# Storing the last tile's output in three parts (256, 128, 128 columns) in place of two (384, 128), in a retention and MLP kernel

## The chip, the cores and the metric

The kernel runs on one core of a Trainium2 chip. The metric is the device time of one execution in microseconds; the median of several executions is given. The profile is that of one further execution, seen by the hardware profiler.

## What is computed

Two layers follow each other. The first is a recurrent retention layer over 4 batches, 8 heads, 768 steps and 64 values a head; the second is a normalised two-matmul MLP with a residual, on 4 x 768 rows of 512 columns. Cut to what matters:

```python
for t in range(S):                                   # 768 steps
    state = gamma * state + einsum('bhd,bhe->bhde', k[:, :, t], v[:, :, t])
    y[:, :, t] = scale * einsum('bhd,bhde->bhe', q[:, :, t], state)
x  = y.transpose(0, 2, 1, 3).reshape(B, S, H * D)    # 4 x 768 x 512
xn = (x - mean(x)) / sqrt(var(x) + 1e-06) * g_ln
out = x + maximum(xn @ w_ch1, 0.0) @ w_ch2           # w_ch1 512 x 2048, w_ch2 2048 x 512
```

## The kernel before

The 3072 rows are cut into 24 tiles of 128 rows, numbered 0 to 23. The recurrence is not run step by step: inside a chunk of 128 steps it is a masked product of q and k, and a state for each chunk carries what went before. The weights are kept in bf16. A row's division by its standard deviation commutes with the MLP's matmuls and the maximum, so it is applied last, as `rstd`.

The order of all work is written out by hand in a long list, `ORDER`, of tokens that are emitted one after the other (the loop at L615). Each engine runs its own instructions in the order in which they are emitted, and waits by semaphores for what it needs from the others. A token such as `z23_1//Y1` means: step `z`, tile 23, part 1, into PSUM bank Y1. A step's engine stands behind the first slash; `st23/A` is a store that ScalarE's queue issues. The steps at the end of the list, around the change, are these:

- `z` (L543): the second matmul of the MLP. For a tile it accumulates 16 matmuls (`ho` 0 to 15) over the hidden 2048 values; each has a weight load of 128 x 128 of `h1` and streams columns `lo` to `hi` of `w2`. It is emitted in four parts of four matmuls.
- `ad` (L550): VectorE reads the bank, multiplies by `rstd`, adds the residual `x_all`, and writes one of six buffers `osb` (number `t + piece`, modulo 6).
- `st` (L557): a DMA, issued by ScalarE's queue, writes those columns of the buffer to the output.

All tiles but the last are one piece of 512 columns. The last tile, 23, is cut at the columns in `CFG["tail"]`; its pieces are written 23, 23b and (where there is a third) 23c in the tokens:

```python
CUTS = CFG["tail"]
COLS = {(t, 0): (0, DM) for t in range(NT - 1)}
COLS.update({(NT - 1, i): c for i, c in enumerate(zip(CUTS, CUTS[1:]))})
...
lo, hi = COLS[t, piece]                              # in z, ad and st alike
for ho in range(4 * part, 4 * part + 4):
    nc.tensor.matmul(bank(("m2", t, piece))[:, 0:hi - lo],
                     lhsT=slot(h1, t // 4)[:, ho, t % 4 * P:(t % 4 + 1) * P],
                     rhs=w2[:, ho, lo:hi], start=(ho == 0), stop=(ho == HO - 1))
```

At the end of the list before the change, TensorE's order is: part 0 of `z23` (bank Y1) in between parts of tile 22 (bank Y0), then tile 20 (bank PD), the last part of tile 21 (bank M), parts 1 to 3 of `z23`, and the 16 matmuls of `z23b` (bank PD). VectorE's is `ad20`, `ad22`, `ad21`, `ad23`, `ad23b`, and ScalarE issues the stores in that order too.

What closes the program is not in the list. Each DMA that SyncE's or ScalarE's queue issues gets one of eight completion counters, in turn (called counter 0 to 7 here). Before the change there are 64 such DMAs, eight for each counter. A DMA waits for the one before it on its counter. When all work is issued, SyncE waits (rows of L643) for these counters, one instruction after the other, in the order 0, 1, ... 7, each together with another semaphore; ahead of them stands one wait for GpSimd's counters. Then the engines meet in a barrier, the semaphores are cleared, and the program ends.

Of the kernel before, what the change touches and what calls it, by code (L numbers as in the profile page):

```python
# [15 lines left out]
 'TX': 8,  # L16
 'groups': [1, 1, 1, 1, 1, 1, 1, 1, 2, 2, 2, 2, 4, 4],
 'pairs': [(8, 9), (10, 11), (12, 13), (14, 15), (16, 17), (18, 19), (20, 21), (22, 23)],
 'tail': (0, 384, 512),
 'slots': {'state': 3,  # L20
           'k0': 7,
           'q0': 4,
# [69 lines left out]
r13_4/A r13_15/A st18/A m13_7//X2 r13_5/A m13_0//X1 r13_7/A m13_8//X0 r13_0/A st17/A st14/A  # L92
st16/A m13_11//X3 r13_8/A r13_11/A z22_0//Y0 m13_10//X2 z21_0//M z21_1 z22_1 r13_10/A z21_2
z22_2 z23_0//Y1 z22_3 z20_0//PD z20_1 z20_2 z20_3 z21_3 ad20 ad22 z23_1 st20/A ad21 z23_2 st22/A
z23_3 st21/A z23b_0//PD ad23 z23b_1 z23b_2 z23b_3 st23/A ad23b st23b/A
""".split()


# [549 lines left out]
```

## Time and profile before

| | |
|---|---|
| median of 3 runs | 211.5 us (210.9 to 212.0) |
| the profiled execution | 211.45 us |
| its span, first to last instruction | 209.7 us |
| TensorE (PE) busy | 202.2 us, 96% of the span |
| VectorE (DVE) busy | 127.7 us, 61% |
| ScalarE (ACT) busy | 76.7 us, 37% |
| GpSimd (POOL) busy | 95.4 us, 45% |
| stores of the output | 23 of 256 KB, one of 192 KB, one of 64 KB |

The span runs from the first to the last instruction of any engine; 1.8 us of the profiled execution's time lie around it. A busy TensorE is not one at its peak: its matmuls overlap, and the start of the next one tells more than the duration of one. SyncE (SP) is never counted as busy; its rows are those of a queue, as are the rows marked with a q behind the engine's name. Times of single rows, where they are given to the nanosecond, are from the trace's instruction and DMA records.

### The profile page before, as it was taken

How to read it: one execution, taken by the hardware profiler on the slowest of the kernel's cores; microseconds unless marked ns; L12 is line 12 of the kernel's file. 1: busy time of each engine (PE TensorE's matmuls, PEld its weight loads, DVE VectorE, ACT ScalarE, POOL GpSimd, SP SyncE). 2: the span in 40 equal slices, each digit the busy share in tenths (PEclk: the TensorE clock that was granted, in tenths of full speed). 3: DMA queues.
4: the chain of work that ended last, by engine and by line, in shares of the span. 5: the costliest groups of instructions: out<-in, count | busy, mean ns of one | idle time of the engine just before them, and what ended most of it. 6: DMA issues, size and time to landing. Idle time of an engine off the chain costs nothing.

```text
span 209.7 us, 4961 instructions
## 1 busy us (share of the span) xinstructions
PE 202.2 (96%) x2007; PEld 131.6 (63%) x2031; DVE 127.7 (61%) x297; ACT 76.7 (37%) x168; POOL 95.4 (45%) x145
## 2 busy tenths in 40 slices
PE   7989999999999999999999999999999999999994
PEld 3568999897558566576587676475545444444443
DVE  4797898596349858579695566978948403110023
ACT  6366654442400514415237124214372512346000
POOL 8997592792695796780587459500000000000000
PEclk9999999999999999999999999999999999999999
DMA  9999999999999999999999999966032400015005
GB/s 130 175 180 180 161 199 163 160 175 154 155 133 169 124 185 124 140 122 210 211 147 171 161 176 106 190 67 143 0 105 100 102 0 3 0 50 202 0 3 200
DMA packets 109946, 27.11 MB, mean 129 GB/s; under 512 B 102625, under 2 KB 106977, under 8 KB 109922
## 3 DMA queue, kind: packets, MB, share of 16 engines
q0 software_dynamic: 77024, 13.37, 87.6%
q1 hardware_dynamic: 28242, 6.85, 25.0%
q10 hardware_dynamic: 4656, 6.56, 10.0%
q8 instruction: 16, 0.26, 0.6%
q14 instruction: 8, 0.07, 0.1%
HBM read 27.30 MB, written 6.29 MB: 160 GB/s over the span
## 4 chain that ended last, share of the span: by engine, by line
PE 54%; DVE 4%; issue 1%
PE X L520 23%; PE M L543 16%; PE Y L543 6%; PE PD L543 4%; DVE trq L386 2%; PE X L395 2%; PE Y L423 1%; PE PD L465 1%; DVE state L475 1%; PE Y L401 1%; DVE osb L550 1%; DVE xn L441 0%; DVE rstd L513 0%
## 5 line engine op out<-in xcount | busy, mean ns | idle before, releaser
L520 PE MATMUL X<-xnt,w 128*128 128x128 bf16 (+2 forms) x896 | 93.8, 257 | 0.0
L531 ACT ACTIVATE h<-X 128x512 bf16<-128x512 f32 x89 | 51.0, 602 | 82.1 <-PE X L520 70.2
L520 PEld LDWEIGHTS <-w 128*128 128x128 bf16 x896 | 66.1, 98 | 20.5 <-issue 0.2
L543 PEld LDWEIGHTS <-h 128*128 128x128 bf16 x400 | 37.4, 98 | 38.2 <-issue 0.3
L543 PE MATMUL M<-w,h 128*128 128x512 bf16 x238 | 59.4, 379 | 1.5 <-issue 0.5
L408 DVE TENSOR_TENSOR asb<-X,mask 128x512 bf16<-128x512 f32 x48 | 30.6, 683 | 11.8 <-PE X L395 11.5
L457 POOL TENSOR_TENSOR vg<-v,vsc 128x512 bf16<-128x512 bf16 x20 | 20.9, 1049 | 9.0 <-DMA v<-in_v_dram 7.3
L550 DVE SCALAR_TENSOR_TENSOR osb<-M,rstd,x_all 128x512 f32<-128x512 f32 x16 | 11.9, 746 | 20.0 <-PE M L543 18.1
L447 ACT CAST x_all<-Y 128x256 bf16<-128x256 f32 (+1 forms) x39 | 14.4, 410 | 25.2 <-DVE xn L441 25.2
L337 POOL DMA_DIRECT2D v<-in_v_dram x24 | 21.9, 912 | 3.6 <-DMA w<-in_moe_w_ch_dram 1.6
L543 PE MATMUL Y<-w,h 128*128 128x512 bf16 (+1 forms) x93 | 21.7, 370 | 0.2
L431 DVE BATCH_NORM_STATS2 bns<-Y 128x6 f32<-128x256 f32 (+1 forms) x39 | 16.3, 454 | 8.2 <-PE Y L423 8.0
L441 DVE SCALAR_TENSOR_TENSOR xn<-Y,mv,gb 128x256 bf16<-128x256 f32 (+1 forms) x39 | 18.6, 512 | 1.2 <-PE Y L423 0.6
L475 DVE TENSOR_TENSOR state<-PD,gch 64x256 bf16<-64x256 f32 x40 | 16.6, 415 | 0.6 <-PE PD L465 0.3
L337 POOL DMA_DIRECT2D qk<-in_q_dram x17 | 15.2, 893 | 1.2 <-issue 1.1
L337 POOL DMA_DIRECT2D qk<-in_k_dram x17 | 15.3, 898 | 0.9 <-issue 0.8
L550 DVE SCALAR_TENSOR_TENSOR osb<-PD,rstd,x_all 128x512 f32<-128x512 f32 (+1 forms) x3 | 1.9, 618 | 20.1 <-remote 17.2
L386 DVE TENSOR_TENSOR trq<-tr,qsc 128x512 bf16<-128x512 bf16 x17 | 10.8, 643 | 3.5 <-DMA tr<-qk 3.3
L564 PE MATMUL PD<-zeros 128*128 128x512 bf16 (+1 forms) x32 | 8.5, 402 | 1.2 <-DVE zeros L250 1.2
L423 PEld LDWEIGHTS <-asb 128*128 128x128 bf16 x192 | 8.0, 98 | 2.7 <-DVE asb L408 0.9
L366 POOL COPY scrap<-qk 1x1 bf16<-1x1 bf16 x28 | 4.9, 176 | 9.8 <-DMA qk<-in_k_dram 8.5
L543 PE MATMUL PD<-w,h 128*128 128x512 bf16 (+1 forms) x46 | 8.4, 324 | 0.1
(75 smaller groups left out, 130.9 us busy)
## 6 DMA issues: line engine op xcount, KB each, us to landing
out_dram<-osb ACTq DMA_DIRECT2D x23, 256.0 KB, 2.4
w<-in_moe_w_ch_dram POOLq DMA_DIRECT2D x8, 512.0 KB, 8.6
v<-in_v_dram POOLq DMA_DIRECT2D x24, 128.0 KB, 6.3
qk<-in_k_dram POOLq DMA_DIRECT2D x17, 128.0 KB, 6.8
qk<-in_q_dram POOLq DMA_DIRECT2D x17, 128.0 KB, 5.7
k<-in_k_dram POOLq DMA_DIRECT2D x6, 128.0 KB, 7.6
q<-in_q_dram POOLq DMA_DIRECT2D x6, 128.0 KB, 7.6
tr<-qk SPq DMA_TRANSPOSE x17, 5.8
```

Source lines behind the costliest of these rows:

```text
L337: nc.gpsimd.dma_start(out=dst, in_=tok[kind][TILES[t]])
L386: nc.vector.tensor_tensor(out=slot(trq, t), in0=x, in1=qsc, op=ALU.mult)
L408: nc.vector.tensor_tensor(out=slot(asb, t)[:, :, par, :], in0=bank(("pa", t, par)).rearrange("p (i t) -> p i t", t=P), in1=mask.rearrange( ...
L431: nc.vector.bn_stats(out=bns[:, t, i, :], in_=x)
L441: nc.vector.scalar_tensor_tensor(out=dst, in0=src, scalar=mv[:, t, 0:1], in1=g, op0=ALU.subtract, op1=ALU.mult)
L447: nc.scalar.copy(out=dst, in_=src)
L457: nc.gpsimd.tensor_tensor(out=slot(vgs, chunk(t)), in0=v_of(t), in1=vsc[:, c, :].unsqueeze(2).to_broadcast([P, H, D]), op=ALU.mult)
L475: nc.vector.tensor_tensor(out=slot(state, chunk(t) - 1)[o, :, o], in0=pd[o, :, o], in1=gch[o, c - 1, :].unsqueeze(2).to_broadcast([D, NPAI ...
L520: nc.tensor.matmul(bank(("mm", g, ho))[:, j * n * P:(j + 1) * n * P], lhsT=w1[:, ko, (ho + j) * P:(ho + j + 1) * P], rhs=x[:, x0:x0 + n, k ...
L531: nc.scalar.activation(out=dst, in_=src, func=AF.Relu)
L543: nc.tensor.matmul(bank(("m2", t, piece))[:, 0:hi - lo], lhsT=slot(h1, t // 4)[:, ho, t % 4 * P:(t % 4 + 1) * P], rhs=w2[:, ho, lo:hi], st ...
L550: nc.vector.scalar_tensor_tensor(out=slot(osb, t + piece)[:, 0:hi - lo], in0=bank(("m2", t, piece))[:, 0:hi - lo], scalar=rstd[:, t:t + 1] ...
```

## The change

The last tile's columns are cut at 256 and 384 in place of 384 alone, and the list gets the steps of the third piece. `z23` has 256 columns then, `z23b` and `z23c` have 128 each. `z23c` accumulates in bank Y0, which tile 22 used before, and its matmuls follow those of `z23b` on TensorE. On VectorE `ad23c` follows `ad23b`, and on ScalarE's queue `st23c` follows `st23b`. `ad23c` writes buffer 1 of `osb`, which tile 19 used before. `st23c` is the 65th DMA of the counters in turn and gets counter 0. On GpSimd and in SyncE's work nothing is added, moved or taken away.

```diff
- 'tail': (0, 384, 512),
+ 'tail': (0, 256, 384, 512),
...
-z23_3 st21/A z23b_0//PD ad23 z23b_1 z23b_2 z23b_3 st23/A ad23b st23b/A
+z23_3 st21/A z23b_0//PD ad23 z23b_1 z23b_2 z23b_3 st23/A z23c_0//Y0 ad23b z23c_1 z23c_2 z23c_3
+st23b/A ad23c st23c/A
```

## The prediction

> **What bounds the kernel now.** I read the page first, then the chain of waits from its end backwards, then the last six microseconds engine by engine, and last the SyncE rows behind the end of the work.
>
> ```profile
> span 209.7 us, 4961 instructions
> PE 202.2 (96%) x2007; PEld 131.6 (63%) x2031; DVE 127.7 (61%) x297; ACT 76.7 (37%) x168; POOL 95.4 (45%) x145
> PEclk9999999999999999999999999999999999999999
> ```
>
> TensorE is busy throughout at the full granted clock. The chain that ended last says the same of the end:
>
> ```profile
> 203.87 1.95 PE Y L543 x12
> 205.82 0.91 PE PD L543 x16
> 206.72 0.02 issue
> 206.75 0.35 DVE osb L550
> ```
>
> Up to 206.7 the second matmul layer (`z`, L543) runs without a pause; the last add (`ad23b`, L550) follows its last matmul. The chain view stops there, but the span runs on to 209.65. The same stretch by windows (PE, PEld, DVE, ACT, POOL busy, granted clock, DMA share, GB/s):
>
> ```profile
> 205.65:206.71 1.06, 1.06 (x18) 0.88 (x15) 0.62 (x1) 0.00 (x0) 0.00 (x0) 1.00 0.99 381
> 206.71:207.13 0.42, 0.00 (x0) 0.00 (x0) 0.35 (x1) 0.00 (x0) 0.00 (x0) 1.00 0.09 29
> 207.13:208.74 1.61, 0.00 (x0) 0.00 (x0) 0.00 (x0) 0.00 (x0) 0.00 (x0) 1.00 0.48 163
> 208.74:209.70 0.96, 0.00 (x0) 0.00 (x0) 0.00 (x0) 0.00 (x0) 0.00 (x0) 1.00 0.00 0
> ```
>
> So the end has four terms in a row: the last matmuls, the add of 128 columns (0.42 with its hand-overs), the last store (1.61), and 0.96 in which no engine and no transfer works. That last one is SyncE's closing waits (L643) and the barrier behind them:
>
> ```profile
> L643 SPq EVENT_SEMAPHORE  x1: 28/28/28, 208.7 to 208.7; - x1
> L643 SPq DRAIN  x1: 13/13/13, 208.8 to 208.8; - x1
> ```
>
> In the trace's rows this last wait runs at 208.740, 17 ns after the last store's final landing mark (208.723); the next instruction starts at 208.807. It is the last of a list that asks for completion counter 0, 1, ... 7 in that order; today the last store owns counter 7, so nothing is left to ask for after it.
>
> **The change part by part.** The sum is made against the profiled execution: 211.45 us, its span 209.65 with 1.80 around it. The median of the runs shown is 211.5, so the two stand together.
>
> *TensorE.* Sixteen matmuls of 384 columns become sixteen of 256, and sixteen of 128 (`z23c`) come in behind `z23b`. Columns in total stay 8192. Start to start in the trace's rows: 162.5 ns for 384 columns (these sixteen), 109 ns for 256 (256 matmuls at L520), 56 ns for 128 (`z23b`). 16 x (109 + 56 - 162.5) = 40 ns. All of it lies on the path: the last matmul ends 0.04 later. The first four of the sixteen stand ahead of `z22_3`, so the adds of tiles 20 to 22 come 4 x 53.5 = 0.21 us earlier. What could go wrong is that thirty-two thin pairs of weight load and matmul in a row do not hold the pace of sixteen. The nearest rows are early in the kernel, where 143 thin matmuls in a row (most of them 128 columns wide, L520) start 54.3 ns apart on average between 30.1 and 37.8 us. Bounds for `z23c`: 16 x 54 = 0.87 below; above, one weight load's whole duration, 98 ns, for each matmul: 1.57, or 0.67 more. I take 0.90, since the rows are the same shape; a gain is excluded, as no column disappears.
>
> The Trainium skill, "TensorE: Matmul & The Clock Gate", section Back-to-back issue gap, speaks against this part: a stream of weight-load and matmul pairs is said to sustain about 81 ns a matmul at 128 columns, and about 131 at 512. This trace has 56 and 216 for the two, so it disagrees in both directions. By the page the sixteen new pairs would take 1.30 us and not 0.90, and the end would come 0.40 later still.
>
> *Does `z23c` wait?* Its bank Y0 was tile 22's, free when `ad22` ends at about 204.2 (204.45 now, less 0.21); `z23c` starts at about 205.7. The cover is 1.5 us of `z23_1` to `z23b`; without it TensorE, with nothing behind, would stand for the remainder. Cost nothing.
>
> *VectorE.* The profile's adds take 0.35 (128 columns), 0.62 (384) and 0.74 (512), about 0.133 per 128 columns, so 256 columns should take 0.48. `ad23` runs from about 205.0 to 205.5, behind `ad21`, which then ends at 204.9; `ad23b` from 205.9 to 206.25; `ad23c` from 206.79 to 207.14. Only the last is on the path, and it is as long as the last one now: 0. Its buffer's earlier store (tile 19) landed at 186.3, so its added wait is over 20 us early, and nothing is queued behind it on VectorE.
>
> *ScalarE's queue.* One more store is issued: `st23` (128 KB), `st23b` and `st23c` (64 KB each) at about 205.5, 206.3 and 207.17, each 0.34 long. They do not meet. `st23c` also waits for the previous owner of its completion counter, tile 17's store, landed at 192.4.
>
> *The last store.* It keeps its size and comes 0.04 later. From issue to its final mark it takes 1.59 now, with its first packets at 207.99 while the 192 KB store's last packet ends at 208.04: an overlap of 0.04. After the change the store ahead is 64 KB and 0.9 earlier, so that overlap goes. Bounds: -0.05 (the overlap and a little) and +0.05 (the marks of one store alone lie 0.18 apart). I take 0.
>
> *SyncE's closing waits.* This is the term that the diff does not show. The 64 transfers of the hardware queues take their completion counters in turn, eight each; the 65th, `st23c`, falls to counter 0. The closing list is unchanged, so the wait for counter 0 comes first among the eight and will hold SyncE until about 208.78 (208.74 + 0.04). Then seven more waits, all long satisfied, must still be run one by one. Satisfied waits on SyncE are in the trace:
>
> ```profile
> L380 SPq EVENT_SEMAPHORE  x2: 28/28/28, 85.9 to 86.0; - x2
> L380 SPq DMA_TRANSPOSE tr<-qk x1: 1470/1470/1470, 86.1 to 86.1; - x1
> ```
>
> Those two waits for two counters each, the form of the closing ones, start at 85.924 and 85.989, and the transpose behind them at 86.056: 65 and 67 ns. Seven at 65 are 0.455. Bounds from the quickest and slowest satisfied wait that I found, 49 ns (95.134 to 95.183, one counter) and 73 (73.549 to 73.622): 0.34 to 0.51. Nothing hides it, because every engine then waits at the barrier behind SyncE; before the change the same seven lie under the stores in flight. A gain is excluded, since the waits run in order.
>
> Sum: 0.04 + 0 + 0 + 0.455 = 0.50. From 211.45 this gives 211.9 us (211.95 unrounded), the span 210.15. That is 0.23% more. The fourth window, 0.96 now, grows to about 1.42; the earlier adds and stores buy nothing, since the end hangs on the last piece, which is as big as before.
>
> **The rivals.**
>
> *Closing waits cost nothing.* If SyncE's list were run otherwise at the end than at 85.9, or its rows overlapped the landing, only the 0.04 and the last store's -0.05 to +0.05 remain: 211.4 to 211.5. For it: the closing list has never been seen with its satisfied part behind the last landing. Against it: every satisfied wait in the trace takes 49 to 73 ns of SyncE's own time. Chance 0.14.
>
> *Slower: TensorE's instruction stream needs one page more.* The page shows the fetches of instructions:
>
> ```profile
> q8 instruction: 16, 0.26, 0.6%
> ```
>
> These are packets of 16384 bytes. Their times follow TensorE: the last comes at 200.04, after 1988 of its weight loads. TensorE's program grows by 32 instructions at its very end, 4077 to 4109. If the tail now falls past the end of what has been fetched, TensorE stands for a fetch: the packets took 0.89 to 1.62 us. With the 0.50 that makes 212.8 to 213.6. It decides as soon as the 32 cross a page, and a fetch is not made ahead. Against it: the fetch at 175.99 fell into a stream of 512-column matmuls that started every 216 ns without a gap, so fetches are made ahead; and the last came with some 100 instructions left, so a page is newly there. Chance 0.09.
>
> **How the numbers follow.** The forecast has 0.77, the first rival 0.14, the second 0.09. The runs shown reach from 210.9 to 212.0, so about 0.5% (1.06 us) is what a measurement of this kernel can tell from no change. The forecast's own range, from its unknown terms, is 211.8 to 212.05 (0.34 to 0.51 for the waits, 0.05 to either side for the store), and the scatter of a median adds some 0.4. The whole range, 211.2 to 212.7, takes in the first rival and the upper bound of `z23c` (0.67 more: 212.6), and leaves out the fetch. Slower by over 0.5% (above 212.56): the second rival's 0.09, and 0.04 of the forecast's for thin pairs at 98 ns and for scatter: 0.13. Faster by over 0.5% (below 210.44): only scatter, 0.03. The rest, 0.84, is within.
>
> **What would show it.** In the changed profile: sixteen 256-column matmuls 109 ns apart and thirty-two of 128 columns 56 apart, the last matmul ending at about 206.75; three adds of about 0.48, 0.35 and 0.35; the last store issued at 207.17 and landed at 208.76; and on SyncE eight closing waits about 65 ns apart behind that landing, where one stands now. I am wrong if those waits do not follow the landing, if TensorE shows a gap after 205 us, or if the last store lands in much less or more than 1.59.

## The result and the profile after

The changed kernel is slower: 212.56 us median of 10 runs (212.02 to 214.26), against 211.37 for the kernel before in the same comparison (210.44 to 212.36). The ratio is 1.0064, 95% interval 1.0037 to 1.0091, which is 0.8 to 1.9 us. (Here and below the ratios leave disturbed executions out, so they need not be those of the medians.) The prediction had 211.9 and called a change of under 0.5% the likely outcome. The page of the changed kernel's profiled execution (212.65 us):

```profile
span 210.9 us, 5021 instructions
PE 203.6 (97%) x2047; PEld 132.2 (63%) x2047; DVE 127.0 (60%) x298; ACT 76.8 (36%) x168; POOL 96.2 (46%) x145
```

The end of its chain of waits (start, duration, what):

```profile
204.00 1.31 PE Y L544 x12
205.31 0.89 PE PD L544 x16
206.20 0.91 PE Y L544 x16
207.11 0.03 issue
207.14 0.35 DVE osb L551
```

TensorE runs through the three pieces without a pause (lines stand one lower than before, as the list grew by a line). The last add is no longer than it was. The windows of the end, with the columns of before: thin matmuls, last add, last store, and what follows its landing.

```profile
205.15:207.14 1.99, 1.95 (x34) 1.77 (x31) 0.93 (x4) 0.00 (x0) 0.00 (x0) 1.00 0.98 370
207.14:207.52 0.38, 0.00 (x0) 0.00 (x0) 0.34 (x1) 0.00 (x0) 0.00 (x0) 1.00 0.45 150
207.52:209.10 1.58, 0.00 (x0) 0.00 (x0) 0.00 (x0) 0.00 (x0) 0.00 (x0) 1.00 0.27 78
209.10:210.87 1.77, 0.00 (x0) 0.00 (x0) 0.00 (x0) 0.00 (x0) 0.00 (x0) 0.71 0.02 5
```

The last window, in which no engine works, was 0.96 and is 1.77. (Its 5 GB/s are one packet of instructions, and its clock of 0.71 is that of an idle TensorE.) In the view of SyncE's waits from 204 us on (total, times, longest), the kernel before shows five waits for stores:

```profile
SPq L643 <- DMA out_dram<-osb: 14.8, 5, 12.1
```

The changed kernel shows one:

```profile
SPq L644 <- DMA out_dram<-osb: 42.7, 1, 42.7
```

SyncE stands at counter 0 for 42.7 us, until the very last store lands, and the seven other waits follow. Its rows between 209.0 and 210.03:

```profile
L644 SPq EVENT_SEMAPHORE  x8: 28/28/28, 209.1 to 210.0; - x8
```

In the trace's rows these eight start at 209.101, 209.573, 209.661, 209.730, 209.792, 209.856, 209.917 and 209.977, and the next instruction at 210.044. The six later steps take 60 to 88 ns, 67 on average, near the 65 that was forecast. The first step alone takes 472 ns, and that was not forecast.

Row by row, the two profiled executions differ by 1.22 us in their spans. I measure from the issue of tile 19's store, a fixed step about 25 us from the end; a store has landed at the last of its sixteen landing marks (us):

| | before | after | difference |
|---|---|---|---|
| start of the span to tile 19's store | 184.320 | 184.668 | 0.348 |
| tile 19's store to the last matmul's start | 22.170 | 22.210 | 0.040 |
| last matmul's start to the last store's issue, with the last add in between | 0.642 | 0.639 | -0.003 |
| last store's issue to its landing | 1.591 | 1.567 | -0.024 |
| landing to the end of the span | 0.928 | 1.790 | 0.862 |

The first line is not the change's: up to that store no engine's instructions differ, and over the nine profiled executions of this study that store comes between 183.6 and 186.9 us. The rest is 0.875 us, 0.41%, inside the measured interval.

### The profile page after: what moved, and what is told of

It reads as the page before. It is cut to its first block, busy times and chain, and to the rows that moved or that the text cites. A ratio compares the mean times of both kernels' runs of the same rounds, so it can differ in the third digit from the quotient of the medians.

```text
span 210.9 us, 5021 instructions
## 1 busy us (share of the span) xinstructions
PE 203.6 (97%) x2047; PEld 132.2 (63%) x2047; DVE 127.0 (60%) x298; ACT 76.8 (36%) x168; POOL 96.2 (46%) x145
## 4 chain that ended last, share of the span: by engine, by line
PE 84%; DMA 8%; POOL 4%; DVE 1%; ACT 1%; issue 0%; POOLq 0%; DVEq 0%; ACTq 0%
PE X L521 36%; PE M L544 25%; PE Y L544 9%; DMA k<-in_k_dram 4%; DMA out_dram<-osb 4%; PE PD L544 4%; PE X L396 3%; PE Y L424 2%; PE PD L466 2%; POOL v L338 1%; PE Y L402 1%; POOL q L338 1%; POOL k L338 1%; POOL w L357 1%; DVE osb L551 1%; POOL vg L458 1%
## 5 line engine op out<-in xcount | busy, mean ns | idle before, releaser
L544 PE MATMUL M<-w,h 128*128 128x512 bf16 x256 | 61.5, 379 | 0.4 <-DVE osb L551 0.4
L544 PEld LDWEIGHTS <-h 128*128 128x128 bf16 x416 | 38.3, 98 | 37.5 <-issue 0.5
L458 POOL TENSOR_TENSOR vg<-v,vsc 128x512 bf16<-128x512 bf16 x20 | 21.4, 1070 | 9.0 <-DMA v<-in_v_dram 8.9
L544 PE MATMUL Y<-w,h 128*128 128x512 bf16 (+2 forms) x112 | 22.0, 341 | 0.0
L387 DVE TENSOR_TENSOR trq<-tr,qsc 128x512 bf16<-128x512 bf16 x17 | 9.9, 589 | 2.5 <-DMA tr<-qk 2.3
L551 DVE SCALAR_TENSOR_TENSOR osb<-Y,rstd,x_all 128x512 f32<-128x512 f32 (+2 forms) x7 | 4.6, 654 | 7.5 <-PE Y L544 4.1
```

What stands on the lines that cost most here:

```text
L458: nc.gpsimd.tensor_tensor(out=slot(vgs, chunk(t)), in0=v_of(t), in1=vsc[:, c, :].unsqueeze(2).to_broadcast([P, H, D]), op=ALU.mult)
L544: nc.tensor.matmul(bank(("m2", t, piece))[:, 0:hi - lo], lhsT=slot(h1, t // 4)[:, ho, t % 4 * P:(t % 4 + 1) * P], rhs=w2[:, ho, lo:hi], st ...
L551: nc.vector.scalar_tensor_tensor(out=slot(osb, t + piece)[:, 0:hi - lo], in0=bank(("m2", t, piece))[:, 0:hi - lo], scalar=rstd[:, t:t + 1] ...
```

## The experiments

Two theories stood against each other. Theory A: the change costs what SyncE's closing list costs, since the last store moved from counter 7, the last in the list, to counter 0, the first of the eight. Rival B: the thin pieces themselves cost it. Within theory A, the 0.41 us by which the first step (0.472) is longer than the usual one (0.06) could be a pause after a long wait (A1) or belong to one place in SyncE's instructions (A2). The tool for all of it is a tiny load that moves the counters on by one. It reads 256 bytes into a row that nobody reads any more; in a token such as `extra3/A`, `j` is the 3 and `eng` the A (ScalarE's queue; S is SyncE's):

```python
...
s = slice(64 * j, 64 * (j + 1))
dma(eng).dma_start(out=grow[:, s], in_=moe_g_ln.rearrange("(o n) -> o n", o=1)[:, s])
```

**Undo the counter alone.**

```diff
 the changed kernel
-... z22_1 r13_10/A z21_2
+... z22_1 r13_10/A extra0/A ... extra6/A z21_2
```

> The changed kernel, with seven small loads (256 bytes each, into a row that nobody reads any more) put on ScalarE's queue at about 195 us, where it is idle for 9 us. They move the last store from completion counter 0 to counter 7, the last of the closing list; nothing else of the tail changes. Theory A (closing list): the time from the last store's landing to the end of the span, 1.79 us in the changed kernel and 0.93 in the one before, falls back to 0.93, and the time to within 0.1 us of the kernel before (ratio 1.000 to 1.001). Rival B (the three thin pieces themselves, on TensorE or upstream of the end): the kernel stays 1.2 us slower, ratio 1.005 to 1.006.

Measured: 211.93 us median, ratio to the kernel before 1.0012, interval 0.9980 to 1.0045. The last add, the last store, and what follows its landing:

```profile
206.08:206.46 0.38, 0.00 (x0) 0.00 (x0) 0.35 (x1) 0.00 (x0) 0.00 (x0) 1.00 0.51 169
206.46:208.04 1.58, 0.00 (x0) 0.00 (x0) 0.00 (x0) 0.00 (x0) 0.00 (x0) 1.00 0.27 80
208.04:208.93 0.89, 0.00 (x0) 0.00 (x0) 0.00 (x0) 0.00 (x0) 0.00 (x0) 1.00 0.00 0
```

The tail's three pieces are all there, and 1.77 has become 0.89. Rival B's 1.005 lies outside the interval, if only just; the rows are clearer: 22.210 us from tile 19's store to the last matmul, as in the changed kernel, and 0.909 from landing to end. Whether the time came back to within 0.1 us cannot be told, as the interval is 1.4 us wide.

**Do the counter alone.**

```diff
 the kernel before
-... z22_1 r13_10/A z21_2
+... z22_1 r13_10/A extra0/A z21_2
```

> The kernel before, with one such small load on ScalarE's queue at about 195 us: its last store moves from counter 7 to counter 0, and the output stays in two parts. Theory A: 0.86 us more between the last landing and the end (1.79 in place of 0.93), ratio 1.004. Rival B: ratio 1.000, since the tail's matmuls, adds and stores are those of before.

Measured: 212.57 us, ratio 1.0058, interval 1.0025 to 1.0091. The same three windows, with two pieces as before and one tiny load 10 us ahead of the last tiles' stores:

```profile
207.34:207.72 0.38, 0.00 (x0) 0.00 (x0) 0.35 (x1) 0.00 (x0) 0.00 (x0) 1.00 0.07 22
207.72:209.32 1.60, 0.00 (x0) 0.00 (x0) 0.00 (x0) 0.00 (x0) 0.00 (x0) 1.00 0.48 164
209.32:211.12 1.80, 0.00 (x0) 0.00 (x0) 0.00 (x0) 0.00 (x0) 0.00 (x0) 1.00 0.01 5
```

From landing to end it is 1.808 us. The effect of the change, but for TensorE's 0.04 us, is reproduced without cutting anything. With 0.473 us between the waits for counters 0 and 1, it repeats the pause too. Theory A stands; rival B does not.

**The last store in the middle of the list.** Three tiny loads on ScalarE's queue in the changed kernel put the last store on counter 3.

```diff
 the changed kernel
-... z22_1 r13_10/A z21_2
+... z22_1 r13_10/A extra0/A extra1/A extra2/A z21_2
```

> The changed kernel with three such small loads: the last store owns counter 3. Counters 0 to 2 are then done before it lands, and four waits stand behind its wait. Theory A1 (SyncE pauses once, 0.41 us longer than the usual 0.06, after the wait that held it): landing to end 0.93 + 0.41 + 4 x 0.064 = 1.60 us. Theory A2 (the pause belongs to one place in SyncE's instructions, between the waits for counters 0 and 1): 0.93 + 4 x 0.064 = 1.19 us.

Measured, one execution of 212.47 us: landing to end 1.175 us, as A2 said; behind the wait for counter 3 the steps are 62, 64, 62 and 59 ns. The pause is again between the waits for counters 0 and 1 (0.472 us), now off the path, while the last store is under way. But that store landed 2.47 us after its issue and not 1.57, which no theory had. The DMA view from 207.4 to 209.7 (40 slices of 0.058 us) shows where the time went:

```profile
DMA  0000000014897400000000000000000000000000
GB/s 0 0 0 0 0 0 0 0 36 151 267 427 214 107 9 0 0 0 0 0 0 0 9 18 27 18 0 0 0 0 0 0 0 0 0 0 0 0 0 0
q14 instruction: 1, 0.01, 1.8%
```

All but a few packets are done by 208.26; then comes a hole, and eight packets of 512 bytes follow from 208.71 to 208.90. The one packet of instructions runs from 208.06 to 208.71, and the eight start when it ends. Fifteen of the sixteen landing marks come by 208.68, the last at 209.53. By this timing, the fetch of instructions held up one sixteenth of the store. That is read from one execution and was not tried apart; the last mark also comes 0.62 us after the last packet, against about 0.4 for the fifteen others, and that part stays open.

**Move SyncE's instructions.** Nine tiny loads issued by SyncE itself, in the kernel before.

```diff
 the kernel before
-... z22_1 r13_10/A z21_2
+... z22_1 r13_10/A extra0/S extra1/S ... extra7/S extra0/S z21_2
```

> The kernel before with nine small loads issued by SyncE behind its last transpose (about 166 us): the last store owns counter 0, and SyncE's closing list stands nine instructions later in its stream. Theory A1 (pause after the wait that held SyncE): landing to end 1.79 us again, with about 0.47 from the wait for counter 0 to the next. Theory A2 (the pause belongs to a place in the stream): the place is passed elsewhere, and landing to end is 0.93 + 7 x 0.064 = 1.38 us.

Measured, one execution of 214.48 us (its tile 19's store comes only at 186.9; a transpose of SyncE that starts at 153.2 in the kernel before starts at 155.8 here, ahead of the first tiny load at 168.6, so the delay is older than the loads, and its cause is open). The last window and SyncE's closing waits:

```profile
211.35:212.69 1.34, 0.00 (x0) 0.00 (x0) 0.00 (x0) 0.00 (x0) 0.00 (x0) 1.00 0.00 0
```

```profile
L648 SPq EVENT_SEMAPHORE  x8: 28/28/28, 211.3 to 211.8; - x8
```

Eight waits in 0.5 us where the changed kernel needed 0.9: the step from counter 0 to counter 1 is 67 ns. Landing to end is 1.358 us, A2's 1.38. The pause is now between SyncE's second and third tiny load: 0.445 us from the end of the one (169.479) to the start of the next (169.924), where the later ones follow within 75 ns. So it belongs to a place in SyncE's instructions: in this stream, as in the others where it can be read, it stands between the 79th and the 80th of SyncE's recorded rows, the second and third behind its last transpose. In each of the nine profiled executions a packet of instructions on queue q14 follows the place by 1.1 to 1.4 us: 1.10 us after the wait for counter 0 in the changed kernel (210.20), 1.41 in the kernel before (193.83), and here at 170.87, 1.39 behind the second load's end. Pause and fetch go together; that the request for the next page of instructions is the pause is an inference, and was not tried by itself.

**What the tiny loads cost.**

```diff
 the kernel before
-... z22_1 r13_10/A z21_2
+... z22_1 r13_10/A extra0/A ... extra7/A z21_2
```

> The kernel before with eight small loads on ScalarE's queue at about 195 us: the counters go once round, and the last store owns counter 7 as before. It shows what the small loads cost by themselves. Both theories: ratio 1.000, landing to end 0.93 us, last matmul, add and store as in the kernel before. If the loads cost something, the gain that the changed kernel made by them was larger than it looked.

Measured: 211.63 us, ratio 1.0021, interval 0.9998 to 1.0043. No cost is shown, and a small one is not excluded by the times. The rows show none behind tile 19's store: 22.170 us to the last matmul as before, 0.908 from landing to end.

**A smaller last piece.**

```diff
 the changed kernel with seven tiny loads
- 'tail': (0, 256, 384, 512),
+ 'tail': (0, 256, 448, 512),
```

> The changed kernel with seven small loads (last store on counter 7) and the cuts at 256 and 448: pieces of 256, 192 and 64 columns. Theory A: with the closing list out of the way the end hangs on the last piece alone. TensorE 0; the add of 64 columns 0.285 us in place of 0.352; the store of 32 KB at most 0.1 less than 1.57 from issue to landing. From the last matmul's start to the end of the span 0.10 to 0.20 us less than the 3.11 of the changed kernel with seven loads; against the kernel before a ratio of 0.9995 to 1.000, too little to be timed. Rival: narrower rows (256 bytes) make the store slower than 1.57, and the gain goes.

Measured: 211.31 us, ratio 1.0017, interval 0.9987 to 1.0047. From the last matmul's start to the end it is 3.064 us against 3.113: 0.05 less, half of the least that was expected. The add is 0.283 and the store 1.503, both as expected, but the store is issued 0.132 after the add in place of 0.032: ScalarE's queue issues the store of the 192 columns until 0.036 after the add, and takes 0.096 more to the next issue. The last matmul starts 0.026 later than with the cuts at 256 and 384, where 0 was expected. Against the kernel before, with TensorE's extra 0.066, the rows come out 0.03 us ahead, far below what can be timed. No version here is shown to beat the kernel before.

**The changed kernel once more.** No edit.

> The changed kernel itself once more, on the same chip as the two others. Theory A: ratio 1.004 to 1.006, landing to end 1.79 us again, with 0.47 us between SyncE's waits for counters 0 and 1 and 0.06 between the later ones. Rival (the 0.47 was a chance of one execution): about 0.07 there, landing to end 1.38.

Measured: 212.35 us, ratio 1.0047, interval 1.0020 to 1.0074; landing to end 1.808 us, 0.472 between the waits for counters 0 and 1, then 59 to 88 ns. The pause is no chance of one execution.

## Why the prediction was right or wrong

- **TensorE, 0.04 forecast:** right to the nanosecond: 22.210 against 22.170 us in every execution of three and of two pieces of this study (256, 128, 128 and 384, 128). Thirty-two thin pairs in a row keep 56 ns; the prediction's 54.3 over 143 matmuls was lower because eight of them, of 64 columns, start about 29 ns apart; the 81 ns that the Trainium skill's "TensorE: Matmul & The Clock Gate" gives for such streams in its section Back-to-back issue gap is not what this kernel shows.
- **Bank, buffer, VectorE, ScalarE's queue, 0 forecast:** right. `ad23` took 0.483, `ad23c` 0.349, and the last store was issued 32 ns after its add.
- **The last store, 0 within 0.05:** right, -0.024.
- **SyncE's closing waits, 0.455 with bounds 0.34 to 0.51:** the mechanism was right and its size was wrong; this is the step that failed. It is 0.862. Of the seven steps behind the wait for counter 0, six are about as sized (0.404 together); the first is 0.472, and 0.41 of that is the pause, a term that the sum did not have (the rows behind the list take 0.014 less than before). Where nine loads of SyncE's put the pause elsewhere, the same list costs 1.358 - 0.928 = 0.430, inside the bounds. I had priced the list by satisfied waits from the middle of the kernel, and had not asked what each place of this very list cost. In the kernel before that pause cannot be read off: counter 1's store landed at 193.03, and the wait for it started at 193.04, which covers a pause that ends at about 192.9. The upper bound of 0.51 came from rows that all lay ahead of the place. (The row of the lower bound, 49 ns at 95.134, was not a satisfied wait: it had held SyncE for 5.6 us. One that was satisfied, at 101.519, took 49 ns too, so the bound stands.) Of the three signs of being wrong that the prediction named, none came; what failed was the 65 ns between the eight waits.
- **The rival "the instruction stream needs one page more":** wrong for TensorE, whose fetches are 16 before and after and whose matmuls show no gap. What goes together with a fetch is the pause on SyncE. A packet on queue q14 at 193.83 was in the trace of before, and the prediction did not ask whose it was; I take it for SyncE's, since it comes with the place in SyncE's instructions in every run. The Trainium skill, "Runtime: NRT & Kernel Launch", section Instruction fetch mechanics, says that each sequencer fetches its next page while running the current one, and that the cost of crossing a boundary of 16 KiB is "mostly hidden". For TensorE this trace agrees (in the kernel before, no gap at the fetches at 175.99 and 200.04); for SyncE, if the pause is its fetch, 0.41 us shows when nothing covers it, with a packet of 8 KB.
- **The sum and the chances:** 0.50 was forecast and the rows give 0.875, so the true place was 0.41% and near the 0.5% line, not at half of it. The interval of the measured 0.64%, 0.37 to 0.91, contains this. That 212.56 us still lies within the whole range is luck: its upper part was made for thin pairs at 98 ns and for scatter, and not for SyncE. The chance of 0.13 for slower by over 0.5% was too small, because the closing list, which had never been seen behind the last landing, got an upper bound of 0.51 and nothing beyond it.

## What to carry to other kernels

Count a kernel's DMAs before adding one at its end: in a program closed like this one, completion counters are taken in turn and are waited for in a fixed order, so one more store can move the last landing from the end of the closing list to its head, and then the whole list runs behind it. Price such a list at the place where it stands, and not by the same instruction elsewhere. And a finer cut of the last output gained nothing here while its last piece kept its size, since the end hung on that piece alone.

## What the hardware showed unexpectedly

- SyncE stopped for about 0.41 us at one place of its instructions, in all eight executions where it can be read (all but that of the kernel before), with a packet of 8 KB of instructions 1.1 to 1.4 us later. With nine more instructions ahead of the closing list, the pause stayed at its place in the stream and fell among these nine.
- Where a fetch of instructions of 0.66 us fell on a store of 64 KB, eight of the store's packets came only when the fetch ended, and the store landed 0.9 us later than otherwise (2.47 in place of 1.57). They met in one execution; that the fetch held the packets back is read from their times.
- The spans from tile 19's store to the last matmul agree to the nanosecond between executions with the same cut, while the first 184 us vary by over 1 us; a change of the tail is read far better there than in the times.
